# An FNet and gated-MLP block: sequence results leave PSUM scaled, and are summed onto their rows in DRAM

## The chip, the core and the metric

The kernel runs on one core of one Trainium2 chip. Its metric is the device time of one execution in microseconds; the time before is the median of three runs. The engines are named as in the profile: PE (matrix), DVE (vector), ACT (scalar), POOL (GpSimd) and SP (sync), each with one instruction stream that it works off in order. POOL and SP also start the DMAs: POOL the gathers by index and the accumulating ones, SP all others.

## The reference

```python
mod = (_silu(c) @ w_mod).reshape(1, 6, 1, 512)
sa, ca, ga, sb, cb, gb = ...                      # six rows of 512
h = layernorm(x) * (1 + ca) + sa                  # x: 2048 x 512
x = x + ga * Real(DFT_seq(DFT_hidden(h)))         # Cr@a - Ci@b
h = layernorm(x) * (1 + cb) + sb
x = x + gb * ((silu(h @ w1) * (h @ w3)) @ w2)     # w1, w3: 512 x 1792, w2: 1792 x 512
```

The DFT matrices are inputs. Every product is made of several fp32r products of high and low parts (`l`, `h2l`, `w1l` are low parts, `bh`, `h2h`, `w1h` high ones).

## The kernel before

**Stages.** First (0 to 93 us in the trace) the rows are normalised, modulated and multiplied by the hidden DFT matrix. Then comes the *sequence stage* (93 to 270 us, matmuls of line 723), then the gated MLP (270 us to the end, matmuls of line 100), which works on transposed rows: column block t (0 to 3) holds 512 of the 2048 sequence positions, `[128, 2, 512]` twice.

**Sequence stage.** `steps` is 16 pairs (j, k): j = 0 makes column blocks 0 and 2, j = 1 blocks 1 and 3, each in eight steps k, with two units m (real, imaginary part; `seq_unit`) to a step. A unit is 24 matmuls (28 in one case) into eight PSUM banks, `acc["x", e]` and `acc["y", e]` for e = 0 to 3. After unit (k, m) = (3, 1), the *turn*, the x banks are read out for block j + 2 (times ga2 = -2 ga); after (7, 1), the *end*, the x banks go to blocks j and j + 2, the y banks to j + 2 alone. Around each unit the loop at line 1473 loads matrices some steps ahead (`load_seq`: one half by SP, the mirrored half by POOL's indirect DMA), has DVE and ACT make their sums and low parts (`prepare_seq`), and has ACT sum squares (`square_seq`), whose tiles are then free for later loads.

**What takes the results.** `xr[t]` holds the rows of x of block t in SBUF (`load_xt`). `residual` adds gate times PSUM to them on DVE. At the end ACT copies the x banks to SBUF (`part`), and `add_sums` adds these later, as background work. `keep` in `ln2` writes the finished rows to DRAM tiles `sums[t, i]`, onto which the MLP's results `y` are added by POOL's accumulating DMA (line 1119).

**Order of work.** All engines' instructions are written in one order. The second normalisation, `ln2(t)`, is a list of small steps in the queue `background`; `advance` takes steps from it after each unit while credits in us for DVE and ACT last and enough of the 50 SBUF slots are free; a pause in the list ends a turn. `drain` puts out whatever is left before an operand that is needed next. In the MLP, `up(g, t)` is four blocks of 12 matmuls, `down` units are six each; the MLP's first parts are `up(0, 0)`, `up(1, 0)`, eight `down` units on block 0 (the `y` of that stretch), then `judge()` (a check of the DFT matrices' symmetry from the summed squares `chk`, on DVE after a memset on POOL), then `up(0, 2)`. `up` for block t first drains until `h2h` and `h2l` of that block are written.

Of the kernel before, what the change touches and what calls it, by code (L numbers as in the profile page):

```python
# [15 lines left out]
P = 128  # L16
N = 512
# [25 lines left out]
def folded(nc, pools, c, cp, wmr, wmc, x, xt, ctr, cti, wdr, wdi, w1, w3, w2, out):  # L43
# [42 lines left out]
    def copy(dst, src, scale=1.0):  # L86
        nc.scalar.activation(dst, src, AF.Copy, scale=scale)  # L87
# [26 lines left out]
    def step(queue, slots, fn, dve=0.0, act=0.0):  # L114
        queue.append((slots, dve, act, fn))
# [200 lines left out]
    def copy_by(dst, src, by):  # L316
        nc.scalar.activation(dst, src, AF.Identity, scale=by)  # L317
# [364 lines left out]
    def square_seq():  # L682

        while squares:
            n, m = squares.popleft()
            k = steps[n][1]
            l, d, junk = lo[n, m], df[n, m], raw.pop((n, m, 1))
            col = square(0, KINDS[m], l[:, 1, :], junk)
            if k == NK // 2:

                nc.gpsimd.memset(chk[0:1, 0, m, col : col + 1], 0.0)
            square(0, KINDS[m], flat(d), junk)
            if n == 0:
                square(1, KINDS[m], bh[n][:, m, :], junk)
            give(junk)
# [3 lines left out]
    def seq_unit(n, m, between=None):  # L699
        j, k = steps[n]  # L700
        l, d, high = lo.pop((n, m)), df.pop((n, m)), bh[n][:, m, :]
        begin, turn, end = (k, m) == (0, 0), (k, m) == (NK // 2 - 1, 1), (k, m) == (NK - 1, 1)
        if begin:
            for e in range(ND):
                acc["x", e], acc["y", e] = bank(2 * e), bank(2 * e + 1)

        def own(t, e):
            return flat(t[k])[:, m * N + e * P : m * N + (e + 1) * P]

        def run(what, e):  # L710
            if what == "x":
                terms = [
                    (own(us, e), high),
                    (own(ul, e), high),
                    (own(us, e), l[:, 0, :]),
                    (own(uh, e), l[:, 1, :]),
                ]
                if k == NK // 2 and m == 1:
                    terms.append((zz[:97, 0, cols(e)], zz[:97, 1, :]))
            else:  # L720
                terms = [(own(us, e), d[:, 0, :]), (own(uh, e), d[:, 1, :])]
            for i, (lhs, rhs) in enumerate(terms):
                nc.tensor.matmul(  # L723
                    acc[what, e],
                    lhs,
                    rhs,
                    start=begin and i == 0,
                    stop=(end or (turn and what == "x")) and i == len(terms) - 1,
                    skip_group_check=what == "x" and k >= NK // 2,
                )  # L730


        order = [(what, e) for what in "xy" for e in range(ND)]
        if (k, m) == (NK // 2, 0):
            order = order[ND:] + order[:ND]
        if between:
            order = [(what, e) for e in range(ND) for what in "xy"]
            order = order[0:1] + order[2:3] + [None] + order[1:2] + order[3:]
        for at in order:
            if at is None:  # L740
                between()
            else:
                run(*at)
        give(l)
        give(d)
        if m == 1:
            give(bh.pop(n))
            if j == 1:
                for t in (uh, us, ul):
                    give(t.pop(k))  # L750

        if turn:
            for e in range(ND):
                residual(j + 2, e, acc["x", e], ga2)
        if end:
            part = [take(F32, "sum") for _ in range(2)]
            for e in range(ND):
                copy(part[e // 2][:, e % 2, :], acc["x", e])
                residual(j + 2, e, acc["y", e], ga)
            for i in range(2):  # L760
                for t in (j, j + 2):
                    step(background, 0, lambda i=i, t=t: add_sums(t, i, part[i]), 1.3)
                step(background, 0, lambda i=i: give(part[i]))

    def add_sums(t, i, src):
        for q in range(2):
            residual(t, 2 * i + q, src[:, q, :], ga)

    xr = {}

    def load_xt(t):
        xr[t] = [take(F32, "xr") for _ in range(2)]
        for i in range(2):
            nc.sync.dma_start(xr[t][i], xt[t, i])

    def residual(t, e, src, gate):
        xs = xr[t][e // 2][:, e % 2, :]
        nc.vector.scalar_tensor_tensor(
            xs, src, gate[:, e : e + 1], xs, op0=OP.mult, op1=OP.add
        )  # L780

    NB = N // 32
    PAIRS = ((0, 2), (1, 3))
    h2h, h2l = {}, {}
    xc, sums = {}, {}

    def ln2(t):  # L790
        v = {}
# [82 lines left out]

        def keep():

            for i in range(2):
                sums[t, i] = dram.tile([P, 2, N], F32, name=f"sum_{t}_{i}")
                nc.sync.dma_start(sums[t, i], xr[t][i])
                give(xr[t][i])  # L880
            xr.pop(t)

        def a9():
            give(v["s"])
# [3 lines left out]
        apart = t != PAIRS[0][0]  # L888
        pause = (0, None, 0.0, 0.0)
        for slots, fn, dve, act in (  # L890
            (2, a1, 1.2, 0.0),
            (0, a1b, 0.7, 0.0),
            (0, rows, 1.3, 0.0),
            (1, partition_sums, 1.0, 0.0),
            (1, a2, 1.5, 0.0),
            (1, lambda: a3(0), 1.2, 0.0),
            *[pause] * apart,
            (1, lambda: a3b(0), 0.0, 1.0),
            (1, lambda: a3(1), 1.2, 0.0),
            *[pause] * apart,  # L900
            (1, lambda: a3b(1), 0.0, 1.0),
            (0, keep, 0.0, 0.0),
            pause,
            (0, a4, 1.2, 0.0),
            (0, a1b, 0.7, 0.0),
            (0, rows, 1.3, 0.0),
            (0, partition_sums, 1.0, 0.0),
            pause,
            (0, a6, 0.0, 2.8),
            pause,  # L910
            (0, a6b, 1.6, 0.0),
            (0, lambda: a7(0), 1.2, 0.0),
            *[pause] * apart,
            (0, lambda: a8(0), 0.0, 1.4),
            (0, lambda: a7(1), 1.2, 0.0),
            *[pause] * apart,
            (0, lambda: a8(1), 0.0, 1.4),
            (0, a9, 0.0, 0.0),
        ):
            step(background, slots, fn, dve * (1.4 if apart else 1.0), act)  # L920
# [128 lines left out]
    def up_block(g, t, q, w):  # L1049
# [18 lines left out]
        else:  # L1068
# [3 lines left out]
            copy(u[:, 0, :], v[:, 1, :])  # L1072
            behind(1, lambda: minus(u[:, 1, :], v[:, 1, :], u[:, 0, :].bitcast(F32)))
            behind(1, lambda: give(v))

    def load_sums(t):
        xr[t] = [take(F32, "xr") for _ in range(2)]
        for i in range(2):
            nc.sync.dma_start(xr[t][i], sums[t, i])

    def store(t, i):
        to = out[t, 2 * i : 2 * i + 2].rearrange("d p n -> p d n")
# [388 lines left out]
    for v, dst in enumerate((ga, sb, cb1, gb)):  # L1471
        mod_columns(v, dst)
    for n, (j, k) in enumerate(steps):
        if k == 2:
            load_xt(j + 2)
        if k == 5:
            load_xt(j)
        for m in range(2):
            if todo and todo[0] == (n, m):
                prepare_some(1, n)  # L1480
            if (k, m) == (NK // 2 - 1, 1):
                drain(lambda: ("mod", 0) in done)
            seq_unit(n, m, last_rows if (n, m) == (0, 0) else None)
            load_some(n + 3)
            prepare_some(2 if n == 0 else 1, n + 2)
            square_seq()
            load_some(n + 4)
            if (j, k, m) == (0, NK - 1, 1):
                for t in PAIRS[0]:
                    ln2(t)  # L1490
                    for i in range(2):
                        chunk_parts(background, t, i, 1)
                sum_parts(background, *pair_sums(background, 0))

            if k % (NK // 2) != NK // 2 - 1 or m == 1:
                advance(2.2 if todo else 5.0)
        if n == len(steps) - 3:
            load_w(("w1", 0))
            load_w(("w3", 0))
        if n == len(steps) - 2:  # L1500
            for w in ("w1", "w3"):
                w_high((w, 0))
                w_low((w, 0))
    give(zz)

# [922 lines left out]
```

## Time and profile before

| | |
|---|---|
| runs | 715.85, 714.74, 714.67 us; median 714.74 |
| profiled execution | span 715.7 us (of the runs' times 715.85 is nearest to it) |
| PE busy | 689.8 us, 96% of the span, 3094 matmuls |
| DVE / ACT / POOL busy | 551.9 / 428.7 / 129.8 us |
| granted PE clock | mean 0.978 of full |
| DMA | 108.93 MB, mean 152 GB/s; accumulating and indirect ones (POOL) 28.8% of 16 engines' span, SP's 27.7% |

Times within the execution count from the start of the span. A busy time says nothing of what an engine waits for; the stretches and the rows of the timeline do, and these stand in the prediction.

### The profile page before, as it was taken

How to read it: one execution, taken by the hardware profiler on the slowest of the kernel's cores; microseconds unless marked ns; L12 is line 12 of the kernel's file. 1: busy time of each engine (PE TensorE's matmuls, PEld its weight loads, DVE VectorE, ACT ScalarE, POOL GpSimd, SP SyncE). 2: the span in 40 equal slices, each digit the busy share in tenths (PEclk: the TensorE clock that was granted, in tenths of full speed). 3: DMA queues.
4: the chain of work that ended last, by engine and by line, in shares of the span. 5: the costliest groups of instructions: out<-in, count | busy, mean ns of one | idle time of the engine just before them, and what ended most of it. 6: DMA issues, size and time to landing. Idle time of an engine off the chain costs nothing.

```text
span 715.7 us, 8791 instructions
## 1 busy us (share of the span) xinstructions
PE 689.8 (96%) x3094; PEld 563.4 (79%) x3094; DVE 551.9 (77%) x873; ACT 428.7 (60%) x700; POOL 129.8 (18%) x147
## 2 busy tenths in 40 slices
PE   7699999999999999999999999999999999999995
PEld 3587888888888888777888788787788888888784
DVE  4889887999899977679997887897666456664663
ACT  4687975455453665646677767667665655656420
POOL 3520073443435000100100101011010101101000
PEclk8599999999999999999999999999999999999998
DMA  8630089878588530442667566376854748447503
GB/s 245 225 116 3 5 289 355 280 257 294 172 312 266 171 142 31 75 76 86 130 164 161 133 148 137 69 127 136 266 115 91 154 76 182 87 91 129 165 1 122
DMA packets 37956, 108.93 MB, mean 152 GB/s; under 512 B 4880, under 2 KB 5136, under 8 KB 37904
## 3 DMA queue, kind: packets, MB, share of 16 engines
q0 software_dynamic: 12352, 43.00, 28.8%
q1 hardware_dynamic: 25552, 65.29, 27.7%
q8 instruction: 26, 0.43, 0.2%
q14 instruction: 26, 0.21, 0.1%
HBM read 76.81 MB, written 33.55 MB: 154 GB/s over the span
## 4 chain that ended last, share of the span: by engine, by line
PE 60%; issue 23%; DVE 6%; DMA 4%; ACT 4%; POOL 2%; SPq 1%; POOLq 0%; ACTq 0%; DVEq 0%
PE bank L100 32%; PE bank L723 25%; POOL sum L1119 2%; PE bank L533 2%; DMA sum<-y 2%; DMA x<-in_x 1%; PE bank L569 1%; DMA wmr<-in_wmr 1%; DVE hl L90 1%; ACT hm L485 1%; PE bank L469 1%; DVE hs L90 1%; ACT y L317 0%; DVE hm L487 0%; ACT ho L87 0%
## 5 line engine op out<-in xcount | busy, mean ns | idle before, releaser
L100 PE MATMUL bank<-hf,w2h 128*128 128x512 f32 (+1 forms) x452 | 140.8, 391 | 1.0 <-ACT y L317 0.7
L1119 POOL DMA_DIRECT2D sum<-y x48 | 41.1, 856 | 390.9 <-ACT y L317 373.1
L100 PEld LDWEIGHTS bank<-hf,w2h 128*128 128x128 f32 x452 | 84.3, 188 | 22.8 <-DVE hf L90 3.4
L100 PE MATMUL bank<-hf,w2l 128*128 128x512 f32 (+1 forms) x226 | 87.6, 388 | 0.0
L317 ACT ACTIVATE y<-bank,gb 128x512 f32<-128x512 f32 x96 | 65.0, 683 | 19.1 <-PE bank L100 18.4
L87 ACT ACTIVATE hf<-v 128x512 fp32r<-128x512 f32 x56 | 35.3, 630 | 67.2 <-DVE v L96 62.6
L93 DVE TENSOR_TENSOR v<-bank,x 128x512 f32<-128x512 f32 x36 | 24.7, 686 | 34.8 <-PE bank L100 34.8
L170 POOL DMA_INDIRECT re<-in_ctr,mirror x32 | 36.5, 1142 | 73.8 <-PE bank L569 37.6
L723 PE MATMUL bank<-bh,us 128*128 128x512 f32 x128 | 49.9, 390 | 0.0
L723 PE MATMUL bank<-bh,ul 128*128 128x512 f32 x128 | 49.8, 389 | 0.0
L723 PE MATMUL bank<-d,us 128*128 128x512 f32 x128 | 49.8, 389 | 0.0
L723 PE MATMUL bank<-d,uh 128*128 128x512 f32 x128 | 49.8, 389 | 0.0
L723 PE MATMUL bank<-l,us 128*128 128x512 f32 x128 | 49.8, 389 | 0.0
L723 PE MATMUL bank<-l,uh 128*128 128x512 f32 x128 | 49.8, 389 | 0.0
L93 DVE TENSOR_TENSOR x<-bank,x 128x512 f32<-128x512 f32 x36 | 24.8, 688 | 32.4 <-PE bank L100 28.7
L100 PEld LDWEIGHTS bank<-hf,w2l 128*128 128x128 f32 x226 | 42.4, 188 | 8.4
L90 DVE TENSOR_TENSOR hf<-v,hf 128x512 fp32r<-128x512 f32 x56 | 38.5, 687 | 12.2 <-ACT hf L87 12.1
L1197 ACT ACTIVATE v<-v 128x512 f32<-128x512 f32 x36 | 22.8, 632 | 38.9 <-DVE v L93 38.9
L87 ACT ACTIVATE x<-bank 128x512 f32<-128x512 f32 x72 | 41.4, 587 | 7.1 <-PE bank L100 6.5
L170 POOL DMA_INDIRECT im<-in_cti,mirror x32 | 35.1, 1096 | 34.4 <-DVE l L90 9.7
L100 PE MATMUL bank<-h2h,w1h 128*128 128x512 f32 x80 | 31.8, 397 | 1.5 <-ACT h2h L87 1.5
L100 PE MATMUL bank<-h2l,w1h 128*128 128x512 f32 x80 | 32.0, 400 | 0.8 <-DVE h2l L90 0.8
(243 smaller groups left out, 1785.7 us busy)
## 6 DMA issues: line engine op xcount, KB each, us to landing
sum<-y POOLq DMA_DIRECT2D x48, 512.0 KB, 5.4
w<-in_w SPq DMA_DIRECT2D x42, 512.0 KB, 4.5
re<-in_ctr SPq DMA_DIRECT2D x32, 256.0 KB, 5.5
im<-in_cti SPq DMA_DIRECT2D x32, 256.0 KB, 4.9
wmc<-in_wmc SPq DMA_DIRECT2D x8, 512.0 KB, 6.9
xr<-in_xt SPq DMA_DIRECT2D x8, 512.0 KB, 7.6
sum<-xr SPq DMA_DIRECT2D x8, 512.0 KB, 6.6
x<-in_x SPq DMA_DIRECT2D x12, 256.0 KB, 4.5
```

What stands on the lines that cost most here:

```text
L87: nc.scalar.activation(dst, src, AF.Copy, scale=scale)
L90: nc.vector.tensor_tensor(out=dst, in0=a, in1=b, op=OP.subtract)
L93: nc.vector.tensor_tensor(out=dst, in0=a, in1=b, op=OP.add)
L100: nc.tensor.matmul(acc, lhs[a], rhs[b], start=first and n == 0, stop=last and n == len(PASSES) - 1, skip_group_check=more,)
L170: nc.gpsimd.indirect_dma_start(dst, None, rows, bass.IndirectOffsetOnAxis(ap=at, axis=0))
L317: nc.scalar.activation(dst, src, AF.Identity, scale=by)
L469: nc.tensor.transpose(turned[k][dt // 2][:, at : at + P], hid_cols(xz[k][:, side, :], dt), anti if side and where(k)[1] else ident,)
L485: nc.scalar.activation(dst, src, AF.Identity, bias=sa, scale=ca1)
L533: nc.tensor.matmul(halves(hb[k])[:, m, :], sides((hh, hl)[a][k])[:, dt, m, :], wu[dt][:, b, m, :], start=False, stop=dt % 2 == 1 and n == ...
L723: nc.tensor.matmul(acc[what, e], lhs, rhs, start=begin and i == 0, stop=(end or (turn and what == "x")) and i == len(terms) - 1, skip_grou ...
L1119: nc.gpsimd.dma_start(sums[t, d // 2], y, accum_op=OP.add)
L1197: behind(k != 0 or q == 0, lambda: nc.scalar.activation(v, src, AF.Silu))
```

## The change

`move` replaces `residual` and `add_sums`: ACT reads each bank out of PSUM with the gate as its scale (at the very end of j = 1, DVE does this for the four y banks), and POOL's DMA adds the tile of four banks' halves onto the rows of x in DRAM. `begin_sums` puts these rows there by a copy from DRAM to DRAM (SP), one step earlier than `load_xt` did. A turn gives two accumulating DMAs, an end six (x tiles onto two blocks, y tiles onto one), so there are 16 new ones. The second normalisation loads its rows from the sums (`load_sums`, SP) with four pauses behind; `keep` no longer writes them out. `moved` and `return_moved` give the tiles back three units later.

```diff
         if turn:
-            for e in range(ND):
-                residual(j + 2, e, acc["x", e], ga2)
+            move({(j + 2,): "x"}, ga2)
         if end:
-            part = [take(F32, "sum") for _ in range(2)]
-            for e in range(ND):
-                copy(part[e // 2][:, e % 2, :], acc["x", e])
-                residual(j + 2, e, acc["y", e], ga)
+            move({(j, j + 2): "x", (j + 2,): "y"}, ga, j == 1)
+
+    def move(what, gate, both=False):
+
+        parts = {}
+        for i in range(2):
+            for to, name in what.items():
+                parts[to, i] = take(F32, "sum")
+            for q in range(2):
+                for to, name in what.items():
+                    dst, e = parts[to, i][:, q, :], 2 * i + q
+                    if both and name == "y":
+                        nc.vector.tensor_scalar(
+                            dst, acc[name, e], gate[:, e : e + 1], None, op0=OP.mult
+                        )
+                    else:
+                        copy_by(dst, acc[name, e], gate[:, e : e + 1])
+        for to in what:
             for i in range(2):
-                for t in (j, j + 2):
-                    step(background, 0, lambda i=i, t=t: add_sums(t, i, part[i]), 1.3)
-                step(background, 0, lambda i=i: give(part[i]))
...
+                for t in to:
+                    nc.gpsimd.dma_start(sums[t, i], parts[to, i], accum_op=OP.add)
+                moved.append([3, parts[to, i]])
...
+    def begin_sums(t):
+        for i in range(2):
+            sums[t, i] = dram.tile([P, 2, N], F32, name=f"sum_{t}_{i}")
+            nc.sync.dma_start(sums[t, i], xt[t, i])
+
+    def load_sums(t):
         xr[t] = [take(F32, "xr") for _ in range(2)]
         for i in range(2):
-            nc.sync.dma_start(xr[t][i], xt[t, i])
...
+            nc.sync.dma_start(xr[t][i], sums[t, i])
...
         def keep():
 
-            for i in range(2):
-                sums[t, i] = dram.tile([P, 2, N], F32, name=f"sum_{t}_{i}")
-                nc.sync.dma_start(sums[t, i], xr[t][i])
-                give(xr[t][i])
-            xr.pop(t)
+            for x in xr.pop(t):
+                give(x)
...
         for slots, fn, dve, act in (
+            (4, lambda: load_sums(t), 0.0, 0.0),
+            *[pause] * 4,
             (2, a1, 1.2, 0.0),
...
-        if k == 2:
-            load_xt(j + 2)
-        if k == 5:
-            load_xt(j)
+        if k == 1:
+            begin_sums(j + 2)
+        if k == 4:
+            begin_sums(j)
...
             square_seq()
+            return_moved()
```

The change also moves the steps of `ln2` among the others. Three places follow as the built programs have them (numbers tell tiles apart).

DVE, end of the sequence stage, before; `xr` on the left is the rows plus gate times a y bank, `h2l` the low parts of block 0, `t` the first sum of block 2's normalisation:

```order
L90 TENSOR_TENSOR h2l_2408<-xc_2216,h2h_2406 128x1024
L90 TENSOR_TENSOR h2l_2436<-xc_2220,h2h_2410 128x1024
L93 TENSOR_TENSOR t_2438<-xr_1277,xr_1278 128x1024
L93 TENSOR_TENSOR t_2438<-t_2438 128x512
L799 STREAM_TRANSPOSE t_2438<-t_2438 128x512
L801 TENSOR_REDUCE r_339_2442<-t_2438 128x16
L90 TENSOR_TENSOR w1l_2446<-w_331_2356,w1h_2444 128x1024
L90 TENSOR_TENSOR w3l_2450<-w_332_2358,w3h_2448 128x1024
L778 SCALAR_TENSOR_TENSOR xr_1980<-bank_264_1801,ga,xr_1980 128x512
```

The same place now; L770 is the read-out of the y banks by `move`:

```order
L90 TENSOR_TENSOR h2l_2440<-xc_2285,h2h_2438 128x1024
L90 TENSOR_TENSOR w1l_2446<-w_333_2372,w1h_2444 128x1024
L90 TENSOR_TENSOR w3l_2450<-w_334_2374,w3h_2448 128x1024
L770 TENSOR_SCALAR sum_2501<-bank_268_1828,ga 128x512
L770 TENSOR_SCALAR sum_2501<-bank_270_1830,ga 128x512
L770 TENSOR_SCALAR sum_2507<-bank_272_1832,ga 128x512
L770 TENSOR_SCALAR sum_2507<-bank_274_1834,ga 128x512
L90 TENSOR_TENSOR h2l_2518<-xc_2323,h2h_2442 128x1024
L90 TENSOR_TENSOR w1l_2545<-w_349_2524,w1h_2543 128x1024
```

The second `h2l` of block 0, an operand of the MLP's first block of matmuls, now stands behind the four read-outs of banks that the sequence stage's last matmuls fill, and `t` of block 2 has gone to a place further on.

DVE, at `judge` (from `sq<-chk` to `bad<-fine`), before; `s`, `w`, `stat` and `xc` are the second half of block 2's normalisation:

```order
L856 RECIPROCAL s_376_2682<-s_376_2682 32x16
L820 COPY w_381_2714<-s_376_2682 32x16 x4
L821 STREAM_TRANSPOSE stat_2517<-w_381_2714 128x512
L96 TENSOR_TENSOR xc_2525<-xc_2525,stat_2517 128x1024
L96 TENSOR_TENSOR xc_2572<-xc_2572,stat_2517 128x1024
L90 TENSOR_TENSOR h2l_2782<-xc_2525,h2h_2780 128x1024
L90 TENSOR_TENSOR h2l_2795<-xc_2572,h2h_2793 128x1024
L979 TENSOR_REDUCE sq<-chk 128x8
```

The same place now:

```order
L1007 TENSOR_TENSOR fine<-sq,own 1x4
L96 TENSOR_TENSOR fine<-fine 1x2
L96 TENSOR_TENSOR fine<-fine 1x1
L1010 TENSOR_SCALAR bad<-fine 1x1
L868 RECIPROCAL s_395_2789<-s_395_2789 32x16
L832 COPY w_395_2813<-s_395_2789 32x16 x4
L833 STREAM_TRANSPOSE stat_2688<-w_395_2813 128x512
L96 TENSOR_TENSOR xc_2708<-xc_2708,stat_2688 128x1024
L96 TENSOR_TENSOR xc_2730<-xc_2730,stat_2688 128x1024
L90 TENSOR_TENSOR h2l_2827<-xc_2708,h2h_2825 128x1024
L90 TENSOR_TENSOR h2l_2831<-xc_2730,h2h_2829 128x1024
```

The reciprocal, with all that follows it in block 2's normalisation, has moved from ahead of `judge` to behind it. On ACT the square root of block 2, its scaling and `h2h` have likewise moved from between the eight `y` to behind the last of them.

POOL, end of j = 0, now; before, the four rows of `im` and `re` at the two ends followed each other with nothing between:

```order
L170 DMA im_1764<-in_cti,mirror 128x512
L170 DMA im_1767<-in_cti,mirror 128x512
L778 DMA sum_0_1464<-sum_1794 128x1024
L778 DMA sum_0_1190<-sum_1794 128x1024
L778 DMA sum_1_1466<-sum_1800 128x1024
L778 DMA sum_1_1192<-sum_1800 128x1024
L778 DMA sum_0_1190<-sum_1795 128x1024
L778 DMA sum_1_1192<-sum_1801 128x1024
L170 DMA re_1821<-in_ctr,mirror 128x512
L170 DMA re_1824<-in_ctr,mirror 128x512
```

Here six accumulating DMAs stand ahead of the mirrored loads of step 11. The last two add onto tiles (`sum_0_1190`, `sum_1_1192`) that the second and fourth are still adding to, and wait for these to land.

More of the change, by code (lines that the diff above doesn't have):

```diff
@@ L765, in add_sums @@
[L765 to L771, printed above, removed]
+            move({(j, j + 2): "x", (j + 2,): "y"}, ga, j == 1)
+    xr, sums = {}, {}
+    moved = deque()
+    def move(what, gate, both=False):
[13 more added lines that the diff above has]
+        for to in what:
+            for i in range(2):
+                for t in to:
+                    nc.gpsimd.dma_start(sums[t, i], parts[to, i], accum_op=OP.add)
+                moved.append([3, parts[to, i]])
@@ L772, in load_xt, with return_moved @@
+    def return_moved():
+        for at in moved:
+            at[0] -= 1
+        while moved and moved[0][0] < 0:
+            give(moved.popleft()[1])
+    def begin_sums(t):
[3 more added lines that the diff above has]
+    def load_sums(t):
         xr[t] = [take(F32, "xr") for _ in range(2)]
         for i in range(2):
-            nc.sync.dma_start(xr[t][i], xt[t, i])
[L776 to L780, printed above, removed]
+            nc.sync.dma_start(xr[t][i], sums[t, i])
@@ L787, in folded @@
     h2h, h2l = {}, {}
-    xc, sums = {}, {}
+    xc = {}
     def ln2(t):
@@ L1074, in up_block @@
             behind(1, lambda: give(v))
[L1076 to L1079, printed above, removed]
     def store(t, i):
@@ L1504, in folded @@
     give(zz)
+    while moved:
+        behind(6, lambda t=moved.popleft()[1]: give(t))
     USED = {"w1": (0.0, 0.5), "w3": (1.2, 0.5), "y": (0.0, 0.6), "own": (0.7, 0.0)}
```

## The prediction

> **What bounds the kernel now.** I read the stretches by stage first: which engine is full where.
>
> ```profile
> core 0: us, PE busy (x) PEld busy (x) DVE busy (x) ACT busy (x) POOL busy (x), PEclk, DMA share, GB/s
> 93.00:270.40 177.40, 177.40 (x788) 146.96 (x787) 159.22 (x224) 95.92 (x185) 63.59 (x62) 1.00 0.75 252
> 270.40:303.10 32.70, 32.62 (x144) 26.67 (x143) 23.73 (x45) 18.93 (x28) 1.86 (x2) 1.00 0.25 52
> 303.10:306.40 3.30, 1.09 (x2) 0.69 (x3) 1.57 (x2) 3.28 (x5) 0.85 (x1) 0.89 1.01 190
> 306.40:345.00 38.60, 38.37 (x163) 31.06 (x162) 33.59 (x57) 20.00 (x28) 2.38 (x4) 0.96 0.30 69
> 345.00:707.60 362.60, 360.00 (x1572) 292.48 (x1570) 258.76 (x404) 222.68 (x327) 36.17 (x43) 1.00 0.58 131
> ```
>
> The sequence stage, whose results the change reroutes, is all matmul: PE is busy for 177.40 of 177.40 us at full clock. DVE, with 159.22 us, is 90% busy there, but nothing waits for it. One short stretch is different, 303.1 to 306.4 us. The waits of PE behind 90 us, longest first, say the same:
>
> ```profile
> PE bank L100 <- ACT h2h L87: 1.5, 1, 1.5
> PE bank L100 <- ACT x L87: 1.2, 3, 0.5
> PE bank L100 <- DVE h2l L90: 0.8, 1, 0.8
> PE bank L100 <- ACT y L317: 0.7, 1, 0.7
> ```
>
> So all that a shorter DVE or ACT could give back behind 90 us is 4.2 us and some half-speed clock. What the change can cost is bounded only by what it puts in front of a matmul. I therefore looked in the timeline at the one place where the second normalisation is already late: `up(0, 2)`, whose first matmul takes `h2h` of block 2 and whose second takes `h2l`.
>
> ```profile
> 302.63 0.39 PE L100 MATMUL bank<-hf,w2l 128*128 128x512 f32 x1
> 304.56 0.50 PE L100 MATMUL bank<-h2h,w1h 128*128 128x512 f32 x1 [1.53 <-ACT h2h L87]
> 305.81 0.79 PE L100 MATMUL bank<-h2l,w1h 128*128 128x512 f32 x1 [0.76 <-DVE h2l L90]
> ```
>
> The last `down` matmul ends at 303.02, the first with `h2l` starts at 305.81: a gap of 2.8 us between the two, with one matmul in it.
>
> **The change part by part: the sequence stage.** Off DVE go 32 scaled additions, on ACT come twelve more read-outs and all of them a scale. Taking work off DVE gives nothing here, since PE waits for none. What could cost is ACT at the end of j = 0: its eight read-outs go x, y by turns, so six of them lie between the first y bank's last matmul, 1.4 us before the unit's end (six matmuls of 0.23), and the last x bank, which the next unit needs twelve matmuls or 2.7 us after that end. At 0.69 us each (the `y` row below, the same read-out with a scale) this is 4.1 - 1.4 = 2.8 us: 0.1 us late at most, and I take 0. For the loads (POOL and SP) see the second rival; I take 0, covered by 19 us.
>
> **The end of j = 1.** Now DVE reads out the y banks ahead of the second `h2l` of block 0. Now the additions of the same place end here:
>
> ```profile
> 269.06 2.73 DVE L778 SCALAR_TENSOR_TENSOR xr<-bank,ga,xr 128x512 f32<-128x512 f32 x4 [1.14 <-PE bank L723]
> 271.71 0.68 DVE L811 COPY q<-r 32x16 f32<-32x16 f32 x4
> ```
>
> and the matmul that takes that `h2l` (the eighth of the MLP) starts at
>
> ```profile
> 271.81 0.39 PE L100 MATMUL bank<-h2l,w1h 128*128 128x512 f32 x1
> ```
>
> No row shows a `tensor_scalar` of a whole bank. At most it costs what the addition does (2.73 us for four); the least is that only the fourth remains behind the last matmul, at 270.4. So DVE is free for `h2l` between 271.1 and 271.7, and `h2l` takes 1.2 us (1.23 in the row below): done by 272.3 to 272.9, and PE waits 0.5 to 1.1 us. I take 1.0, by the addition, which reads the same bank.
>
> **In front of `up(0, 2)`.** Here the order matters. The reciprocal of block 2 and all behind it have gone behind `judge`, and `judge` needs the POOL memset, which stands behind the fourth accumulating DMA of `y`, which needs the eighth `y`. So nothing of this chain can start before the last `down` matmul is over. The rows that price it, from ACT, DVE and POOL:
>
> ```profile
> 256.05 2.93 ACT L867 ACTIVATE xc<-xc,sb,cb 128x512 f32<-128x512 f32 x4 [1.85 <-DVE xc L96]
> ...
> 298.33 1.52 ACT L867 ACTIVATE xc<-xc,sb,cb 128x512 f32<-128x512 f32 x2 [1.37 <-issue]
> ...
> 303.45 1.05 ACT L87 ACTIVATE h2h<-xc 128x1024 fp32r<-128x1024 f32 x1
> 304.39 0.69 ACT L317 ACTIVATE y<-bank,gb 128x512 f32<-128x512 f32 x1
> ```
>
> ```profile
> 295.26 0.24 DVE L856 RECIPROCAL s<-s 32x16 f32<-32x16 f32 x1 [0.93 <-ACT s L853]
> ...
> 297.02 2.36 DVE L96 TENSOR_TENSOR xc<-xc,stat 128x1024 f32<-128x1024 f32 x2
> 304.53 1.23 DVE L90 TENSOR_TENSOR h2l<-xc,h2h 128x1024 fp32r<-128x1024 f32 x1 [5.16 <-ACT h2h L87]
> ...
> 307.58 0.42 DVE L979 TENSOR_REDUCE sq<-chk 128x8 f32<-128x256 f32 x1 [0.30 <-POOL sq L978]
> ...
> 310.61 1.20 DVE L90 TENSOR_TENSOR xc<-xc,xc 128x1024 f32<-128x1024 f32 x1
> ```
>
> ```profile
> 300.73 0.87 POOL L1119 DMA_DIRECT2D sum<-y  x1 [3.06 <-ACT y L317]
> 303.28 0.85 POOL L1119 DMA_DIRECT2D sum<-y  x1 [1.69 <-ACT y L317]
> 306.50 0.86 POOL L1119 DMA_DIRECT2D sum<-y  x1 [2.38 <-ACT h2h L87]
> 307.04 0.51 POOL L978 MEMSET sq<- 128x96 f32 x1
> ```
>
> ```profile
> DMA to landing us min/median/max: 3.5/5.4/8.9
> ```
>
> Counted from the end of the last `down` matmul. (1) The eighth `y` is out at 0.7. (2) The fourth accumulating DMA also waits until the second, onto the same tile, has landed. That one's last `y` is made 5.4 us earlier (four units of six matmuls) and read out, behind a square on ACT, some 4.4 us earlier; with the median landing of 5.4 us POOL is free to issue at 1.0. In the trace now these two DMAs start 5.77 us apart, 300.73 and 306.50. (3) The memset is done 1.05 after that issue (306.50 to 307.55): 2.05. (4) `judge` takes 3.03 (307.58 to 310.61): 5.1. (5) Reciprocal to the first `xc`, 295.26 to 297.02, is 1.76: 6.85. (6) First `xc` until ACT starts on it, 297.02 to 298.33, is 1.3: 8.15. (7) Four scalings, 2.85 of the 2.93 until the next can start: 11.0. All four stand ahead of `h2h` on ACT. (8) `h2h`, 303.45 to 304.53 where DVE has it, 1.08: 12.1. (9) `h2l` until PE starts, 304.53 to 305.81, 1.28: 13.35. The square root and its table load on ACT lie beside (3) and (4).
>
> This takes the place of the 2.8 us gap: +10.55 us. With the 1.0 from the end of j = 1, which moves everything behind it, +11.55.
>
> The Trainium skill ("DMA: Bandwidth & Descriptors", Rules for kernel authors) says that an accumulate reads its destination and writes it later, so that another one onto the same bytes must wait for the first one's semaphore. The 5.77 us between the two starts agree; it speaks against this change, as it makes a chain of the accumulations onto one tile.
>
> **Behind it.** The eight additions of `add_sums` (block 1 and 3) leave DVE, where nothing waits for them: 0. The later places of the normalisations move by a few instructions; PE's waits there, 1.2 + 0.7 us above, may go or come again. I take 0, with -2 to +2 for the range.
>
> **The rivals.**
>
> *Faster: the load off DVE lets block 2's normalisation finish in time.* The gap of 2.8 us then closes, and the half clock behind it goes too: 306.4 to 345 had 0.96 of the clock, 1.5 us lost. That is 714.74 - 4.3 = 710.4 us. For it speaks DVE's 90% in the sequence stage. It decides if ACT has `h2h` of block 2 ahead of the last `y`. Against it: in the written order `h2h` stands behind all eight, and engines keep their order.
>
> *Slower still: the sequence stage starves.* Six accumulations at the end of j = 0 come on top of the loads:
>
> ```profile
> 180.00:232.00 52.00, 52.00 (x231) 43.09 (x230) 49.91 (x75) 22.02 (x45) 23.83 (x24) 1.00 0.77 252
> ```
>
> ```profile
> q0 software_dynamic: 576, 2.10, 78.9%
> ```
>
> The second row is the four `y` accumulations in the 16 us from 296 on: 78.9% of 16 us, 3.2 us of all engines' time for each. Six are 19.3 us, on top of 0.77 x 52 = 40 us: 59 us of transfers for 52 us, so loads fall up to 7 us behind. Besides, POOL holds the mirrored loads of step 11 until the second and the fourth accumulation have landed, some 10 us. Against that stands the lead of
>
> ```profile
> 186.23 1.39 POOL L170 DMA_INDIRECT re<-in_ctr,mirror  x1 [4.50 <-PE bank L723]
> ```
>
> ```profile
> 201.09 0.69 DVE L90 TENSOR_TENSOR l<-re 128x512 fp32r<-128x512 f32 x1
> ```
>
> From issue to use on DVE are 14.9 us, of which about 6 are the transfer (5.77 for the accumulation above); PE takes the unit at 215 (ten units of 24 matmuls and four more ahead of 270.2), 10 us after DVE has made it. 9 + 10 us are 19 us of cover against 7 + 10 us. It decides beyond 19 us; 5 us over would give 731.3 us.
>
> *The clock stays halved for longer.* The gap of 13 us contains a whole window of idleness, the one now does not. If PE resumes at half speed for twice the time of now, another 1.5 us is lost: 727.8 us. The Trainium skill ("TensorE: Matmul & The Clock Gate", Part 1) has the clock fall to half after an idle window of about 3.4 us, and rise only after a busy one; how the windows lie decides between one and two. The 0.96 agrees with one half-speed window.
>
> *No change:* the compiled order is not what runs, or a cover I missed: 714.7.
>
> **How the numbers follow.** The span was 715.7 us, 1 us above the median of the runs, 714.74; the sum of +11.55 gives a span of 727.3 and a time of 714.74 + 11.55 = 726.3 us. Its own range: below, 0.5 instead of 1.0 at the end of j = 1, a landing of 3.5 (the eighth `y` then decides, -0.3) and -2 behind: 723.5. Above, a landing of 8.9 (+3.5) and +2: 731.8. Chances: this forecast 0.72; clock 0.10, within its range; starvation 0.12; faster 0.04; no change 0.02. The range from 723.0 to 732.0 leaves out the last two and most of what lies above in starvation. A measurement of this kernel tells about 0.2% from no change; faster 0.04, same 0.02, slower 0.94.
>
> **What would show it.** Right: PE without waits from 93 to 270 us; one wait of about 1 us for `h2l` (DVE) near 272; a gap of about 13 us from 304 to 317 with `judge` on DVE in it, and POOL's memset ahead of that; everything behind shifted alike. Wrong: `h2h` of block 2 made before the last `y`; waits of line 723 for `l`, `d` or `bh`; or a loss that lies behind 345 us.

## The result, and the profile after

The changed kernel takes 734.48 us (median of six runs, 731.05 to 737.08), the kernel before 715.26 us in the same comparison. The ratio is 1.026 (95% interval 1.0235 to 1.0285). The forecast was 726.3 us, 723.0 to 732.0: the sign is right, the size is not, and the place of the difference is the sequence stage, for which the forecast had 0.

First the times at which PE passes some places, from the timeline of each kernel. Before (the rows around `up(0, 2)` stand in the prediction):

```profile
93.08 0.40 PE L723 MATMUL bank<-bh,us 128*128 128x512 f32 x1
...
270.22 0.39 PE L100 MATMUL bank<-h2h,w1h 128*128 128x512 f32 x1
...
707.22 0.28 PE L100 MATMUL bank<-hf,w2l 128*128 128x256 f32 x1
```

After:

```profile
90.85 0.40 PE L723 MATMUL bank<-bh,us 128*128 128x512 f32 x1
...
274.78 0.39 PE L100 MATMUL bank<-h2h,w1h 128*128 128x512 f32 x1
...
308.51 0.39 PE L100 MATMUL bank<-hf,w2l 128*128 128x512 f32 x1
...
321.94 0.80 PE L100 MATMUL bank<-h2h,w1h 128*128 128x512 f32 x1 [13.04 <-ACT h2h L87]
323.20 0.80 PE L100 MATMUL bank<-h2l,w1h 128*128 128x512 f32 x1 [0.46 <-DVE h2l L90]
...
724.14 0.28 PE L100 MATMUL bank<-hf,w2l 128*128 128x256 f32 x1
```

The difference of each stretch follows from these rows:

| stretch | before, us | after, us | difference | forecast |
|---|---|---|---|---|
| start to the first matmul of line 723 | 93.08 | 90.85 | -2.23 | 0 |
| sequence stage: to the first matmul with `h2h` | 177.14 | 183.93 | +6.79 | 0 |
| to the end of the last `down` matmul (302.63 + 0.39; 308.51 + 0.39) | 32.80 | 34.12 | +1.32 | +1.0 |
| gap: to the first matmul with `h2l` in `up(0, 2)` | 2.79 | 14.30 | +11.51 | +10.55 |
| to the last matmul | 401.41 | 400.94 | -0.47 | 0 |
| from there to the end of the span (715.7; 733.1) | 8.48 | 8.96 | +0.48 | 0 |

The sum is 17.40 us, the difference of the two spans. The first row is not an effect of the change: over the twelve profiled executions of this case that stretch lasted 90.37 to 93.08 us. Without it the loss is 19.6 us, near to the 19.2 us between the medians.

Now the same two views of the kernel after as of before. By stretches, cut where PE waits (columns as before):

```profile
90.85:225.40 134.55, 134.55 (x598) 111.19 (x596) 103.47 (x137) 72.93 (x147) 61.34 (x63) 1.00 0.94 305
225.40:235.20 9.80, 6.12 (x15) 4.79 (x15) 8.73 (x11) 6.98 (x14) 7.19 (x7) 0.65 1.01 323
235.20:274.80 39.60, 39.60 (x176) 32.71 (x175) 29.75 (x52) 23.20 (x36) 4.67 (x7) 1.00 0.50 159
274.80:308.90 34.10, 33.10 (x145) 26.75 (x143) 23.55 (x38) 15.56 (x22) 5.45 (x7) 1.00 0.71 134
308.90:323.20 14.30, 0.80 (x2) 0.29 (x2) 8.61 (x30) 7.45 (x10) 1.04 (x2) 0.67 0.48 80
323.20:327.50 4.30, 4.30 (x11) 3.42 (x12) 2.21 (x2) 0.93 (x1) 0.00 (x0) 0.52 0.01 4
```

And the longest waits of PE from 90 us on:

```profile
PE bank L100 <- ACT h2h L87: 13.0, 1, 13.0
PE bank L723 <- ACT sum L317: 3.7, 1, 3.7
PE bank L100 <- DVE h2l L90: 1.5, 2, 1.0
```

Two of these were forecast: 13.0 us for `h2h` and 1.0 us for `h2l` (the second row of 0.5 is the one in front of `up(0, 2)`). The 3.7 us at 225 us are new, and with them comes a stretch at half clock: the granted clock is 0.65 from 225.4 to 235.2 us. DVE did lose work in the stage, as said, and PE got nothing from it.

**What PE waits for at 225 us.** It is the turn of j = 1. The unit behind it has done its y matmuls and needs an x bank that ACT has still to read out. ACT and PE in the timeline:

```profile
226.55 0.63 ACT L188 ACTIVATE re<-l 128x512 f32<-128x512 f32 x1 [2.05 <-DVE d L90]
...
228.38 2.41 ACT L317 ACTIVATE sum<-bank,ga 128x512 f32<-128x512 f32 x4
...
229.10 0.80 PE L723 MATMUL bank<-bh,us 128*128 128x512 f32 x1 [3.68 <-ACT sum L317]
```

ACT has the read-outs (228.38) in its order behind squares of a unit that PE does not need yet, and the square at 226.55 waited for DVE's `d` of the same unit. DVE was late because a matrix came late: it stands still for 12.30 us until the first mirrored matrix of step 11 is there, and is hardly idle from then to the turn. Before, it took up the same step at 201.09 without a wait (row in the prediction).

```profile
209.01 0.69 DVE L90 TENSOR_TENSOR l<-re 128x512 fp32r<-128x512 f32 x1 [12.30 <-DMA re<-in_ctr,mirror]
```

Back to the queue that fetches it, POOL:

```profile
182.63 1.74 POOL L778 DMA_DIRECT2D sum<-sum  x2 [0.39 <-ACT sum L317]
191.66 0.86 POOL L778 DMA_DIRECT2D sum<-sum  x1 [7.30 <-DMA sum<-sum]
198.29 0.85 POOL L778 DMA_DIRECT2D sum<-sum  x1 [5.78 <-issue]
199.45 1.08 POOL L170 DMA_INDIRECT re<-in_ctr,mirror  x1 [0.30 <-issue]
```

The fifth and sixth accumulating DMA of the end of j = 0 (the y tiles) wait until the second and the fourth, onto the same rows, have landed. For the sixth the row says only `issue`; the landings of the first four, which the view of line 778 from 180 to 190 us gives, show it:

```profile
DMA to landing us min/median/max: 7.5/11.2/14.6
```

The fourth, issued at 183.2, is the one that took 14.6 us, to 197.8, and the sixth follows at 198.29. All that POOL has behind them waits too (the *hold* below): the mirrored load of step 11, issued at 186.23 before, goes out at 199.45.

**The gap in front of `up(0, 2)`.** Its chain is the one of the prediction, step for step, counted from 308.90:

```profile
310.85 0.85 POOL L1125 DMA_DIRECT2D sum<-y  x1 [2.47 <-DMA sum<-y]
311.39 0.50 POOL L989 MEMSET sq<- 128x96 f32 x1
311.92 0.42 DVE L990 TENSOR_REDUCE sq<-chk 128x8 f32<-128x256 f32 x1 [2.19 <-POOL sq L989]
...
314.94 0.23 DVE L868 RECIPROCAL s<-s 32x16 f32<-32x16 f32 x1
...
316.69 2.36 DVE L96 TENSOR_TENSOR xc<-xc,stat 128x1024 f32<-128x1024 f32 x2
318.01 2.93 ACT L879 ACTIVATE xc<-xc,sb,cb 128x512 f32<-128x512 f32 x4 [6.77 <-DVE xc L96]
320.85 1.99 ACT L87 ACTIVATE h2h<-xc 128x1024 fp32r<-128x1024 f32 x2
```

The fourth accumulating DMA is issued at 1.95, not 1.0; from there each step has the length forecast (memset done at 2.99, `judge` over and reciprocal at 6.04, first scaling at 9.11, `h2h` at 11.95, PE at 13.04 and 14.30).

### The profile page after: what moved, and what is told of

Its sections match the earlier page's. It is cut to its first block, busy times and chain, and to the rows that moved or that the text cites. A ratio compares the mean times of both kernels' runs of the same rounds, so it can differ in the third digit from the quotient of the medians.

```text
span 733.1 us, 8801 instructions
## 1 busy us (share of the span) xinstructions
PE 689.1 (94%) x3094; PEld 562.4 (77%) x3094; DVE 534.1 (73%) x845; ACT 436.6 (60%) x712; POOL 141.9 (19%) x163
## 4 chain that ended last, share of the span: by engine, by line
PE 62%; issue 11%; DVE 9%; DMA 8%; ACT 6%; POOL 2%; SPq 1%; POOLq 0%; ACTq 0%; DVEq 0%
PE bank L100 48%; PE bank L723 12%; DMA sum<-sum 3%; DMA im<-in_cti,mirror 2%; PE bank L533 1%; DMA wmr<-in_wmr 1%; DMA sum<-y 1%; ACT xc L879 1%; ACT hm L485 1%; SPq L227 1%; DVE hl L90 1%; PE bank L569 1%; POOL im L170 1%; DVE xc L96 1%; POOL re L170 1%
## 5 line engine op out<-in xcount | busy, mean ns | idle before, releaser
L170 POOL DMA_INDIRECT im<-in_cti,mirror x32 | 33.6, 1049 | 22.1 <-issue 6.1
```

The lines of the kernel that those rows point to most:

```text
L170: nc.gpsimd.indirect_dma_start(dst, None, rows, bass.IndirectOffsetOnAxis(ap=at, axis=0))
```

## The experiments

The stage is from the first matmul of line 723 to the first with `h2h`; the gap from the last `down` matmul to the first with `h2l` in `up(0, 2)`; the last column from the first matmul of line 723 to the last of the MLP, which leaves the uneven start out. The lengths are of the one profiled execution. The times of 715.26 and 734.48 us come from one comparison; each other row was compared with runs of the kernel before of its own (medians 714.97 to 716.75 us), so the ratios and the lengths compare better than the times. Rows with (1) rest on a single run. The stages of changed, judge early and early load, in which the accumulations stand in the same places, differ by 0.4 us; so closely can a length be read, except where chance decides on the clock (last part).

| kernel | time, us (runs) | ratio to before | stage | gap | to the last matmul |
|---|---|---|---|---|---|
| before | 715.26 (6) | 1 | 177.14 | 2.79 | 614.14 |
| changed | 734.48 (6) | 1.026 (1.0235 to 1.0285) | 183.93 | 14.30 | 633.29 |
| judge early | 734.6 (4) | 1.0251 (1.0218 to 1.0285) | 183.56 | 11.55 | 631.83 |
| early load | 726.74 (4) | 1.0142 (1.0108 to 1.0175) | 183.62 | 7.75 | 626.19 |
| y accumulations later | 726.92 (4) | 1.0152 (1.0117 to 1.0187) | 177.60 | 14.28 | 626.35 |
| all accumulations later | 727.87 (4) | 1.016 (1.0127 to 1.0193) | 179.11 | 13.84 | 628.57 |
| hold only | 732.17 (1) | | 181.18 | 14.31 | 629.94 |
| later, more bytes | 731.06 (1) | | 181.26 | 14.15 | 629.69 |
| turns on DVE | 730.59 (1) | | 180.33 | 13.94 | 629.29 |
| three edits | 726.83 (5) | 1.0147 (1.0126 to 1.0168) | 192.07 | none | 623.36 |
| repaired | 723.72 (4) | 1.0114 (1.0098 to 1.013) | 177.88 | 4.57 | 619.45 |
| before, no pauses | 713.57 (6) | 0.996 (0.9945 to 0.9975) | 177.11 | none | 611.09 |

**The y accumulations later.** The two DMAs are put into a list, `held`, and issued three units later:

```diff
+                later_on = len(what) > 1 and len(to) == 1 and not both
                 for t in to:
-                    nc.gpsimd.dma_start(sums[t, i], parts[to, i], accum_op=OP.add)
-                moved.append([3, parts[to, i]])
+                    if later_on:
+                        held.append([LATE, t, i, parts[to, i]])
+                    else:
+                        nc.gpsimd.dma_start(sums[t, i], parts[to, i], accum_op=OP.add)
...
+    LATE = 3
```

`later_on` holds for the y tiles at the end of j = 0.

> At the end of j = 0 the two accumulating DMAs of the y banks are issued by POOL three units later, behind the mirrored loads, so POOL does not hold those loads until the earlier sums have landed. The same transfers, the same bytes. Theory hold (PE starved at 225 us because POOL, in order, kept the mirrored loads behind two accumulations that wait for earlier ones): the mirrored loads of step 11 are issued by 186 us instead of 199.5, the wait of 3.7 us and the half clock behind it go, the sequence stage is 177 to 178 us instead of 183.9, the time 6 us less. Theory bytes (the 16 DMA engines are full from 182 to 228 us, and six accumulations of 3.2 us of all engines are too much wherever they stand): the stage stays at 182 us or more, with PE's wait only moved.

The stage falls to 177.60. POOL's order shows why: the loads go out right behind the x accumulations, and the y ones find their rows landed.

```profile
183.50 1.72 POOL L782 DMA_DIRECT2D sum<-sum  x2 [0.39 <-ACT sum L317]
185.52 1.08 POOL L170 DMA_INDIRECT re<-in_ctr,mirror  x1 [0.30 <-issue]
...
200.42 1.91 POOL L794 DMA_DIRECT2D sum<-sum  x2 [0.36 <-DMA re<-in_ctr,mirror]
```

Same bytes, 6.3 us less: without the hold they cost 0.5 us over the stage of before. They do use up the cover: the load issued at 185.52 lands 14.6 us later (4.1 us before), DVE waits 2.61 us for it, and PE waits 0.15 us at the turn.

**All six later.** The four x accumulations also wait one unit.

> As the run before, but the four accumulating DMAs of the x banks are issued one unit later as well, behind the mirrored loads of that unit; POOL then waits at no place for ACT's read-outs ahead of a load. Theory hold: at least as short a sequence stage as with the y accumulations alone, 177 to 178 us; if the x ones held the loads and the y ones did not, only this run shows it. Theory bytes: still 182 us or more.

179.11 us, above the 177 to 178 expected and 1.5 us more than with the y ones alone; PE waits twice for a read-out, 0.7 us each, one of them already at 139.70 us, ahead of anything that was edited. So moving the x accumulations as well gains nothing that this run shows.

**The hold without most of the bytes.** The changed kernel, with the y accumulations in their old place but cut to 64 of 512 columns:

```diff
+                small_add = len(what) > 1 and len(to) == 1 and not both
                 for t in to:
-                    nc.gpsimd.dma_start(sums[t, i], parts[to, i], accum_op=OP.add)
+                    n = N // 8 if small_add else N
+                    nc.gpsimd.dma_start(
+                        sums[t, i][:, :, :n], parts[to, i][:, :, :n], accum_op=OP.add
+                    )
```

> The changed kernel, but the two accumulating DMAs of the y banks at the end of j = 0 carry an eighth of their columns (64 of 512 positions; the rest of these sums is left out). They stand where they stood and still wait for the earlier accumulation onto their rows, so POOL is held nearly as long with 5.6 us of all 16 DMA engines less to move. Theory hold: POOL issues the mirrored loads of step 11 only at 193 to 199 us (199.5 in the changed kernel, 185.5 with the y accumulations three units later), PE waits at the turn of j = 1, the stage is 181 to 184 us. Theory bytes: the loads catch up by the turn, the stage is 177 to 178.5 us.

```profile
183.20 1.72 POOL L780 DMA_DIRECT2D sum<-sum  x2 [0.40 <-ACT sum L317]
192.31 1.10 POOL L780 DMA_DIRECT2D sum<-sum  x1 [7.39 <-DMA sum<-sum]
198.94 1.08 POOL L780 DMA_DIRECT2D sum<-sum  x1 [5.53 <-issue]
200.32 1.08 POOL L170 DMA_INDIRECT re<-in_ctr,mirror  x1 [0.30 <-PE bank L723]
```

The load goes out at 200.32 and the stage is 181.18. With an eighth of the y bytes the hold costs 4.0 us over before; their other seven eighths cost 2.75 on top of it (183.93 - 181.18). Of these 2.75 us, 1.5 are wait (3.68 against 2.16 us); most of the rest is a second stretch of half clock (last part).

**More bytes without the hold.** The y accumulations later, and SP adds two copies of 512 KB at the end of j = 0:

```diff
+            if (j, k, m) == (0, NK - 1, 1):
+                for i in range(2):
+                    extra = dram.tile([P, 2, N], F32, name=f"extra_{i}")
+                    nc.sync.dma_start(extra, xt[1, i])
```

> The third run (y accumulations three units later) with two copies of 512 KB from DRAM to DRAM added by SP at the end of j = 0; nothing reads them. Theory hold: POOL's queue is not held, the loads have some slack, the stage stays within 1 us of 177.6. Theory bytes (the DMA engines, full from 190 to 230 us, were just short of starving PE): each copy costs about 3 us of all engines, so the loads come 6 us later and the stage grows to 181 us or more.

181.26 us, 3.7 more than without the copies: the theory that bytes do not matter falls. POOL's mirrored load goes out at 186.33 here, and PE still waits 2.4 us at the turn. The load that is late at the turn is one of SP's: DVE, which waits 3.10 us for it, takes it up at 223.79, 131.3 us into the stage, and without the copies at 220.73, 129.0 us into it. That is 2.2 us later, and the wait at the turn has grown by 2.3 (0.15 to 2.44). So more transfers are enough, with POOL's queue free. The copies stand in SP's own queue ahead of its loads; whether their place there counts or their share of the DMA engines, this run does not separate. The stage had a few us of cover, and the hold, the bytes, or both use it up.

**The turns on DVE.** In `move`, the four read-outs of a turn become `tensor_scalar` on DVE.

> The changed kernel with the four read-outs of each turn on DVE (a multiplication by the gate) instead of ACT; the accumulations are as they were. In the changed kernel PE waited 3.7 us at the turn of j = 1 for ACT's read-out of an x bank, and ACT stood in a square that waited for DVE, which waited for late mirrored loads. Theory late loads: the read-outs on DVE stand behind the same late steps, the wait becomes 2 to 3.7 us, the stage 182.5 to 184. Rival (ACT's order made the wait, the late loads alone would have cost nothing): the wait goes, the stage is 177 to 178.5.

```profile
227.86 0.47 PE L723 MATMUL bank<-bh,us 128*128 128x512 f32 x1 [2.93 <-DVE sum L770]
```

The result lies between the two. The wait stays (2.93 instead of 3.68), so late loads are enough for it; but this time no half clock follows, and that is the larger part of the 3.6 us gained. The shorter wait alone did not spare it, since still shorter ones in other runs did not; where the wait fell in time did (last part), so another execution may lose it again.

**`judge` early.** `judge()` moves from behind the eight `down` units to in front of them.

> judge() stands ahead of the eight down units instead of behind them, nothing else. Theory chain: the gap in front of up(0, 2), 14.3 us from the end of the last down matmul to the first matmul with h2l, is made of ACT's square root (done 2.35 us after the last down matmul), then judge on DVE until 6.0, then the reciprocal. Without judge the reciprocal starts at 2.5 instead of 6.0: the gap falls by 3.5 us to about 10.8, and the time by 3.5 to 4 us. Rival (ACT sets the gap by its own order, judge only fills an idle DVE): the gap stays at 14 and the time where it was. The sequence stage (first matmul of line 723 to the first with h2h, 183.9 us against 177.1 before) stays long in either.

The gap falls by 2.75 us, to 11.55. The square root comes later here (done 3.3 us after the last `down` matmul, 2.35 in the changed kernel), because `judge` now takes DVE's time ahead of that normalisation, and PE waits 0.7 us for a `y`. The stretch of the `down` units is 1.0 us longer, and the time does not move: 734.6 us. Of the two forecasts the gap bears out the first, the time the rival.

**Block 2's rows early.**

```diff
-            (4, lambda: load_sums(t), 0.0, 0.0),
-            *[pause] * 4,
+            (4 * (t != 2), lambda: t == 2 or load_sums(t), 0.0, 0.0),
+            *[pause] * (4 * (t != 2)),
...
             (0, keep, 0.0, 0.0),
+            *[(4, lambda: load_sums(2), 0.0, 0.0)] * (t == 0),
```

> The rows of block 2 are loaded from the sums right after block 0 has given its own rows back, and the four pauses ahead of block 2's normalisation are gone; blocks 0, 1 and 3 as they were. Theory (the steps of block 2 were late because load_sums and its four pauses put them behind, and so the order put the whole chain behind the last down unit): the reciprocal, the products and three of the four scalings now stand ahead of judge and of the last y, the gap in front of up(0, 2) falls from 14.3 to 4 to 5 us, close to the 2.8 of before, and the time by 9 to 10 us. Rival (the gap is made by the wait for POOL's accumulations and memset, wherever the steps stand): the gap stays over 10 us. The sequence stage stays near 184 us in either.

The gap falls from 14.30 to 7.75 us and the stretch to the last matmul by 7.1. The late load and its pauses, taken together, are shown as what put the chain behind the last `down` unit. That it is not 4 to 5 us lies with `judge` again, which now stands ahead of `h2l` on DVE:

```profile
313.94 1.99 ACT L87 ACTIVATE h2h<-xc 128x1024 fp32r<-128x1024 f32 x2
314.00 0.42 DVE L991 TENSOR_REDUCE sq<-chk 128x8 f32<-128x256 f32 x1 [2.42 <-POOL sq L990]
...
317.01 2.34 DVE L90 TENSOR_TENSOR h2l<-xc,h2h 128x1024 fp32r<-128x1024 f32 x2
318.27 0.80 PE L100 MATMUL bank<-h2l,w1h 128*128 128x512 f32 x1 [2.65 <-DVE h2l L90]
```

**Three edits together.** The y accumulations later, `judge` behind `up(0, 2)`, block 2's rows early, and one pause instead of four ahead of block 0.

> Three edits together: y accumulations of j = 0 issued three units later (as in the third run), the rows of block 2 loaded right after block 0 has given its own back and one pause instead of four ahead of block 0's normalisation, judge() behind up(0, 2). In the new order h2h of block 2 stands ahead of the last four y on ACT and both h2l of block 0 ahead of DVE's four read-outs. Theory (all of the loss lies in the three places: hold of the loads, wait at the end of j = 1, chain in front of up(0, 2)): stage 177.6 us, no wait for h2h or h2l near 272 or in front of up(0, 2), no half clock there: from the first matmul of line 723 to the last matmul of the MLP 610 to 612 us, against 614.1 before and 633.3 after; time 711 to 713 us. Rival (taking work off DVE and adding 8.4 MB of transfers costs something everywhere, so places we have not named lose too): 616 us or more, time over 717.

The MLP does what was expected: no gap, and from its first matmul to its last 431.29 us (714.50 - 283.21) against 437.00 before. But the stage takes 192.07 us:

```profile
218.21 1.23 DVE L93 TENSOR_TENSOR t<-xr,xr 128x1024 f32<-128x1024 f32 x1 [8.96 <-DMA xr<-sum]
```

and among the waits of PE:

```profile
PE bank L723 <- ACT sum L317: 12.8, 1, 12.8
```

Block 0's rows, loaded at 195 us behind the accumulations, landed up to 20.7 us later, and DVE, in order, waited 9 us for them with the next units' operands behind. The pauses that look like idle turns in the list are the cover of this load. The forecast had not priced it.

**The repaired kernel.** As that, with the four pauses ahead of block 0, and without the extra ones for block 2.

> The changed kernel with the repairs that worked: y accumulations of j = 0 three units later, the rows of block 2 loaded right after block 0 has given its own back, no extra pauses for block 2, judge() behind up(0, 2), and the four pauses ahead of block 0 kept, so that its load has landed by its use. Theory: stage 177.6 us, wait of 1 us for h2l near 272, a gap of 3 to 4 us in front of up(0, 2) since h2h stands right behind the last y; from the first matmul of line 723 to the last of the MLP 615 to 617 us against 614.1 before, time 717 to 719: the change as it stands can be brought to the time of before but not below it by these edits. Rival: something else of the change costs, and it stays over 620 and 722.

Stage and gap come back to 177.88 and 4.57 us, but the times do not come to the 717 to 719 expected: 723.72 us, and 619.45 us from the first to the last matmul in the fastest run. Against before, 0.7 us are the stage, 1.3 the `h2l` near 272, 1.8 the gap, 0.7 the half clock behind it and 0.8 lie later, where PE waits 2.9 us for `x` instead of 1.2. The runs reach from 721.53 to 724.81 us; where the others lose is not known. The change was not brought to the time of before.

**The kernel before, without pauses.** What the gap in front of `up(0, 2)` is worth with the old way of adding:

```diff
-        apart = t != PAIRS[0][0]
+        apart = t not in PAIRS[0]
```

> The kernel before, with one edit: block 2's normalisation does without the four extra pauses that stand in its list of steps. In the new order h2h of block 2 stands ahead of the second y on ACT instead of behind the seventh. Theory (the 2.8 us gap in front of up(0, 2) and the half clock behind it, 1.5 us, are all that a better order can give back there): the gap closes, no matmul over 0.5 us behind it, time 3 to 4.3 us less than before, about 712.5. Rival (the earlier scalings and h2h now hold ACT's read-outs of the first y banks, and PE waits there instead): under 1 us gained.

`apart` also scales the credits that DVE is charged for block 2's steps (1.4 times before, once now), so the edit is not of the pauses alone. 713.57 us, ratio 0.996 (0.9945 to 0.9975): 0.4% less than before. From the first to the last matmul it is 3.05 us less, the low end of the theory. The gap is gone, and the rival has its part: the scalings ahead of the first `y` make PE wait 1.9 us.

```profile
298.85 0.50 PE L100 MATMUL bank<-hf,w2h 128*128 128x512 f32 x1 [1.93 <-ACT y L317]
...
304.52 0.39 PE L100 MATMUL bank<-hf,w2l 128*128 128x512 f32 x1
304.75 0.39 PE L100 MATMUL bank<-h2h,w1h 128*128 128x512 f32 x1
304.98 0.39 PE L100 MATMUL bank<-h2l,w1h 128*128 128x512 f32 x1
```

## Why the prediction missed

**The step that failed** is in the rival on starvation, "it decides beyond 19 us": 9 + 10 us of cover against 7 + 10 us of delay, and so 0 for the loads in the sum, a chance of 0.12 for the rival, and 5 us in its example. It happened, and cost 6.8 us in the changed kernel: 3.7 of wait and about 3 of half clock. Three things in it were wrong.

- The delay. Counted from the first matmul of line 723, the first mirrored load of step 11 was issued 15.4 us later than before (108.60 against 93.15) and landed 9.5 us after its issue instead of 4.1: 20.8 us in all, where 17 had been reckoned. For the hold, "some 10 us" had been taken; from the fourth accumulation (183.2) to the sixth (198.29) POOL was held 15. Landings of 5.4 us came from the y accumulations of the MLP, where the DMA engines are 0.25 to 0.58 busy; here they are full (0.99 from 180 to 232 us), and the median landing was 9.9 us.
- The cover. DVE took the load up 10.2 us later than before (118.16 against 108.01 us into the stage). "PE takes the unit 10 us after DVE has made it" counts only the wait for operands, and that part just held: PE waited for none. The read-out of the turn, which the change moves to ACT, stands there behind squares of a later unit, and so needs that unit's operands first. The part on read-outs priced the end of j = 0, where ACT is free, and passed over the turn.
- The price. A wait of 3.7 us in a full stage was followed by a stretch at half clock; the rival's example of 5 us had none.

That transfers and hold draw on the same cover was right: the transfers alone cost 0.5 us, the hold with an eighth of the y bytes 4.0, both 6.8 us.

**The gap** was right in its chain and 0.95 us short in step (2). The second accumulating DMA landed in 5.4 us, as taken, and was issued 4.28 us ahead of the end of the `down` matmuls (304.62), near the 4.4 taken; it had landed at 1.1. The fourth was issued 0.8 us behind that landing, for which the sum had nothing; what these 0.8 us are, no row shows. All later steps had the lengths that the trace of before gave. The 5.77 us between two starts, which the prediction read as a wait for a landing, were not one: that row ends its wait with `h2h` on ACT. In the changed kernel such a wait is seen, 2.47 us for `DMA sum<-y` at 310.85.

**The end of j = 1** was right: 1.0 us of wait for `h2l`, four `tensor_scalar` in 2.73 us as the four additions; with the clock 1.3 us.

**The clock rival** did not come at this place: the 13 us gap was followed by 5.6 us of slow matmuls (321.94 to 327.50), the wait of 2.8 us before by 3.5 (305.81 to 309.27). From the first `h2l` on this is 0.4 us more, where the rival had 1.5.

**Nothing for a shorter DVE** was right, and so was the sign. Of the three signs named for a wrong forecast, waits of line 723, one came, with another name: `sum` instead of `l`, `d` or `bh`.

## What to carry to other kernels

Where an engine issues DMAs in order, a DMA that waits for the landing of an earlier one holds all loads behind it: price the hold by landings measured under the load that it will meet, and put the dependent DMA behind the loads, not the loads behind it. For the cover of a late load, follow every instruction that is queued behind its user on each engine, the reading out of the accumulators too, and not only the operand itself. A pause in a hand-made order can be the cover of a transfer; take it out only where the trace shows the data landed.

## What the hardware showed that was not expected

The half clock came after waits of 3.68 us (changed), 2.44 us (later, more bytes) and 2.16 us (hold only), and not after one of 2.93 us (turns on DVE). So the length of a wait does not decide alone. In each of the twelve profiled executions, all changes of the granted clock lie whole multiples of 3.41 us apart, which cuts the execution into cells of that length. The cells at the turn, in the changed kernel, hold only and turns on DVE (columns as in the prediction):

```profile
224.93:228.34 3.41, 0.50 (x3) 0.07 (x1) 3.38 (x5) 1.73 (x4) 2.65 (x3) 1.00 0.97 402
228.34:231.75 3.41, 2.65 (x6) 2.15 (x7) 2.48 (x4) 3.41 (x9) 2.01 (x3) 0.50 1.00 286
```

```profile
225.15:228.56 3.41, 1.25 (x6) 0.74 (x5) 2.47 (x5) 2.93 (x7) 1.98 (x3) 1.00 0.91 335
228.56:231.98 3.42, 3.42 (x10) 2.64 (x9) 3.38 (x4) 3.39 (x8) 2.56 (x3) 0.50 0.95 239
```

```profile
222.98:226.39 3.41, 1.95 (x9) 1.29 (x7) 3.31 (x6) 1.36 (x5) 2.80 (x3) 1.00 1.22 493
226.39:229.80 3.41, 1.94 (x9) 1.62 (x10) 3.41 (x7) 1.76 (x4) 2.19 (x3) 1.00 0.87 234
```

A cell in which PE was busy for 0.50 or 1.25 us (1.35 in later, more bytes) was followed by one at half clock. The wait of 2.93 us fell across two cells, with 1.95 and 1.94 us of work, and the clock stayed. How much work a cell needs, these figures bound only roughly. The half clock lasted one cell in hold only and two in the changed kernel, and each full cell costs PE some 1.7 us (an estimate, half of 3.41).

The Trainium skill ("TensorE: Matmul & The Clock Gate", Part 1) names an idle window of about 3.4 us for the fall to half, at free-running times. The cells of 3.41 us, which lie differently in each execution, agree; that a wait well under a whole window can halve the clock is what these rows show, and the measurement decides. In a stage that is full, such a wait can so cost about twice its length: 3.68 us of wait went with 6.8 us of loss, 2.16 with 4.0, but 2.93 with 3.2.

An accumulating DMA landed much later beside the sequence stage's loads than in the MLP. From the DMA issues of the changed kernel (KB each, median us to landing), first the six at the end of j = 0 (174 to 212 us), then the page's row of the `y`:

```profile
sum<-sum POOLq DMA_DIRECT2D x6, 512.0 KB, 9.9
```

```profile
sum<-y POOLq DMA_DIRECT2D x48, 512.0 KB, 5.4
```
